# Half passes of three units in one group, and one pool of six banks, in a fused spectral filter and gated MLP kernel

## The chip, the cores and the metric

The kernel runs on one core of one Trainium2 chip. A core has five engines that run side by side and wait for each other by semaphores: TensorE (matrix multiplications), VectorE and ScalarE (elementwise work), GpSimd, and SyncE, which issues the DMA transfers. TensorE writes its results into eight accumulation banks (128 partitions of 512 float32 each, the kernel's PSUM pool); VectorE and ScalarE read them out of there. The metric is the time of one execution in device microseconds.

## The reference

```python
xn = layernorm(x)                                   # x: 2048 x 448, over the last axis
A  = irfft2(rfft2(xn) * (w_r + 1j * w_i))           # 2D FFT filter
gate, up = xn @ W_gate, xn @ W_up                   # 448 -> 1792
B  = ((gate * (gate > 0)) * up) @ W_down            # 1792 -> 448
return x + A + B
```

All in float32. The kernel keeps that accuracy with float16 multiplications by splitting each operand into a high and a low half and adding three products (high by high, high by low, low by high).

## The kernel before

**The MLP.** The 1792 hidden features are 14 blocks f of 128, in three groups (`GROUPS` = 5, 5, 4 blocks). The 2048 rows are four chunks q of 512, worked in the order 0, 2, 1, 3 (`CHUNKS`). A *unit* is one block of one chunk: its gate and its up matrix of 128 x 512 results, each in a bank of its own. With the halves, the 448 contracted features need 10 full passes (128 contracted rows, `gu_full`, L714) and one half pass (64 contracted rows, `gu_half`, L721) for gate, and as many for up. So a unit is 20 full and 2 half passes. The half pass of gate uses the upper 64 rows of the array (`TOP[0]`), that of up the lower 64 (`TOP[1]`), and the two run side by side as a pair.

Half passes are collected: units are taken two at a time. The first of the two, here called the *head*, does its 20 full passes (`gu_unit`), and then `gu_halves` opens the second unit's tile, the *mate*, does the mate's two half passes as its first contributions and the head's two as its last. The mate's 20 full passes follow later and complete it. `tc.high_priority` and a dependency that only fixes an order (`NOSYNC`) keep the four half passes together.

After a unit, ScalarE applies the ReLU to gate (`gu_relu`, L751), VectorE multiplies by up (`gu_times`, L755), ScalarE makes the float16 high part (`gu_hi`, L759), VectorE the low part (`gu_lo`, L763). The unit's banks are free when `gu_relu` and `gu_times` have read them. When all blocks of a group have been done for a chunk, four *down* units follow (`dn_mm`, L782), one for each 128 rows; each adds up 15 or 12 passes in a bank, and VectorE adds the result to `xy` (`dn_post`, L788). The list `units` puts the four down units behind the next pair that ends.

**Banks.** `gu` is a tile of two banks with two buffers, `dn` a tile of one bank with two buffers, and `fx` (for the transforms) another with two: 4 + 2 + 2 = 8.

**Weights.** Each block's weights are loaded, scaled and split by `w_sq`, `w_sum`, `w_scale`, `w_hi` (L664) and `w_lo` (L668), four gate/up units before the block's first unit. A half pass reads the last tile of the low part. The transposed activations `Tq[q]` come by transposing DMAs (`ln_dma`, L332).

**The spectral part** is the *background* work: a list `bg` of some 400 small steps (normalization, DFT matmuls `f_dft` L360, `f_sdft` L392, `i_sdft` L611, `i_ddft` L632, butterflies on VectorE, swap transfers `swap`, L553 reading them). It is spread over the units by a planner: a unit offers VectorE time (`room`) of share x `took` (4.55 us for a gate/up unit, 0.56 us per block for a down unit) less what the unit itself needs (`fixed`, 1.37 or 0.68 us and the weights' work). A bisection finds the share with which the rooms of all units from `RAMP` up to `last_gu` take in the whole list. `run_bg` then issues as many steps behind each unit as its room allows.

**The order of the work.** The first units, up to `hp4` and what stands around it, follow an order written out by hand (`OPENING`). Behind it a list scheduler orders each engine's instructions when the program is built, by priority (order in the program, with `gu_post` and `dn_post` 400 places ahead, `at` steps 200, the half passes behind the first 2000) and by when it expects operands and banks to be there; on the chip every engine then runs its list in order. So a matmul that waits for a bank holds up all matmuls behind it.

Of the kernel before, what the change touches and what calls it, by code (L numbers as in the profile page):

```python
# [21 lines left out]
XW = 4 * GW  # L22
# [119 lines left out]
def tile_gfnet_reglu(ctx: ExitStack, tc: tile.TileContext, x, xr, wgu, wd, wf, wrow, ident, c_fd, c_fm, c_im, c_row, c_id,  # L142
# [9 lines left out]

    def fx():
        return psum.tile([128, 512], F32, name="fx", bufs=2)

# [178 lines left out]
    def ln_tp(n2, tiles):  # L334
        if n2 not in tp:
            tp[n2] = fx().bitcast(F16).rearrange("p (a b) -> p a b", b=128)
        for a in tiles:
            P.transpose(tp[n2][:, a, :], tt[n2][:, a, :], id_t)
# [8 lines left out]


    zps, eo, X, Xh, yps, cur = {}, {}, {}, {}, {}, {}

    def f_dft(n2):
        q, j = n2 % 4, n2 // 4
        js = slice(128 * j, 128 * (j + 1))
        ps = fx()
        T = Tq[q]

        for r in range(4):
            a, b = (r, 4 + r) if r < 3 else (7, 8)
            for i, (t, c) in enumerate(((a, 0), (a, 1), (b, 0))):
                P.matmul(ps[:, r * GW:(r + 1) * GW], T[:, t, js], fd_t[:, r, c], start=(r == 0 and i == 0),  # L360
                         stop=True, skip_group_check=True)
        zps[n2] = ps
# [25 lines left out]
    def f_sdft(n2):  # L388
        y = yps[n2] = fx()[:, 0:XW].rearrange("p (g c k) -> p g c k", g=4, c=2)
# [177 lines left out]
    def row_dft(d):  # L567
        y = state["rowps"] = fx()
# [35 lines left out]
    def i_sdft(n2):  # L604
        ps = fx()
        v, m = vt[n2 % 8][:, n2 // 8], im_t[n2 % 8][:, n2 // 8]
# [19 lines left out]
    def i_ddft(n2):  # L626
        ps = fx()
        h = pgh[n2]
# [79 lines left out]
    def gu_open(f, q):  # L708
        hps[f, q] = psum.tile([128, 2, 512], F32, name="gu", bufs=2)

    def gu_full(f, q, gs, cs, start, stop, seq=SEQ):
        for g in gs:
            for i, (a, b) in enumerate(seq):
                last["P"] = P.matmul(hps[f, q][:, g, cs], wt[f, g][:, a, :], Tq[q][:, b, cs],  # L714
                                     start=(start and i == 0), stop=(stop and i == len(seq) - 1)).ins

    def gu_half(f, q, g, start, prev):


        rows, b = TOP[g]  # L720
        m = P.matmul(hps[f, q][:, g, 0:512], wt[f, g][rows, 7, :], Tq[q][rows, b, :], start=start, stop=not start).ins  # L721
        if "opened" in state:
# [5 lines left out]

    def gu_unit(f, q, mate):

# [5 lines left out]
        gu_full(f, q, gs, cs, True, False)  # L736
        gu_halves(f, q, mate)

    def gu_halves(f, q, mate):
        gu_open(*mate)  # L740
        m = last["P"]
        for i in range(4):
            with tc.high_priority(offset=2000 if i else 0):
                m = gu_half(*((f, q) if i > 1 else mate), 1 - i % 2, i < 2, m)
        opened.add(mate)

    g1s = {}

    def gu_relu(f, q):
        g1s[f, q] = mt([128, 512], F32, "g1", 3)  # L750
        last["A"] = A.activation(g1s[f, q], hps[f, q][:, 0, :], AF.Relu, scale=2.0 ** -22).ins  # L751

    def gu_times(f, q):
        g1 = g1s[f, q]
        last["V"] = V.scalar_tensor_tensor(g1, hps[f, q][:, 1, :], 2.0 ** -22, g1, op0=OP.mult, op1=OP.mult).ins  # L755

# [209 lines left out]
    units += pend  # L966
    mates = {u: v for u, v in zip(gseq[::2], gseq[1::2])}
    first = {}
# [77 lines left out]
    def gu_slab(f, g):  # L1046
        if f % 2 == 0 and g == 0:
            gu_open(f, q)
        gu_full(f, q, (g,), slice(0, 512), f % 2 == 0, f % 2 == 1)

    for f in groups[0]:
# [6 lines left out]
        for tag, fn in (("re", gu_relu), ("tm", gu_times), ("gh", gu_hi), ("gl", gu_lo)):  # L1058
            piece(f"{tag}{f}", fn, f, q)
        if f % 2 == 0:  # L1060
            piece(f"hp{f}", gu_halves, f, q, mates["gu", 0, f, q][2:])
        for g in range(2):
# [11 lines left out]
    with tc.manual_schedule(engines={mybir.EngineType.PE, mybir.EngineType.DVE, mybir.EngineType.Activation,  # L1074
                                     mybir.EngineType.SP, mybir.EngineType.Pool}):
        A.activation(mt([128, 1], F32, "root"), eps, AF.Sqrt)
        G.memset(warm, 0.0)
        wps = psum.tile([128, 512], F32, name="dn", bufs=2)
        gu_open(0, q)
# [17 lines left out]

    last_gu = max(gus) - 6
    lo, hi = 0.3, 1.2
# [13 lines left out]
    for i, u in list(enumerate(units))[len(groups[0]):]:  # L1113
        is_gu = u[0] == "gu"
        if is_gu:
            _, g, f, q = u
            run_bg(until=marks["T", q])
            gu_unit(f, q, (mates.get(u) or (0, 0, None, None))[2:])
        else:
# [70 lines left out]
```

## Time and profile before

| what | value |
|---|---|
| time, median of three runs | 448.41 us (447.95 to 448.84) |
| span of the profiled execution, first to last instruction | 446.9 us |
| TensorE clock granted | 1.000 of full |
| TensorE busy | 437.4 us, 98% |
| VectorE busy | 373.0 us, 83% |
| ScalarE busy | 178.7 us, 40% |

For the profiled execution only its span is given; the 1.5 us between it and the median of the runs lie outside the first and last instruction. In the rows that the prediction shows, a group of instructions is named by its line, engine, operation and tiles (result <- operands), then shapes, the count, the busy time, the mean length of one in ns, and the idle time of the engine just before them with what ended it. In rows of a timeline the first number is the start and the second the length in us from the first start to the last end. Matmuls overlap in their pipeline, so lengths add up to more than the time that passes: the difference of two starts is what a stretch takes.

### The profile page before, as it was taken

The page shows a single profiled execution, that of the slowest core. Times are in us where ns is not written, and L with a number is a line of the kernel's source. Part 1 is how long each engine was busy: PE and PEld are TensorE (multiplying, and loading weights), DVE is VectorE, ACT ScalarE, POOL GpSimd, SP SyncE. Part 2 cuts the span into 40 slices and gives each one's busy share as a digit, 9 for nine tenths or more (in the row PEclk, how much of TensorE's full clock was granted, in tenths as well). Part 3 has the DMA queues.
Part 4 walks back from the last instruction along what each step waited for, and adds up shares of the span by engine and source line. Part 5 has one row for each costly group of instructions (what it writes and reads, how often), then busy time and mean ns, then how long its engine had stood idle before and what let it go on. Part 6 is the DMA issues. An engine that isn't in the chain of part 4 may idle for free.

```text
span 446.9 us, 7057 instructions
## 1 busy us (share of the span) xinstructions
PE 437.4 (98%) x2618; PEld 217.6 (49%) x2618; DVE 373.0 (83%) x801; ACT 178.7 (40%) x365; POOL 35.5 (8%) x100
## 2 busy tenths in 40 slices
PE   7999999999999999999999999999999999999996
PEld 2543545444545444444444444444444456546564
DVE  5988696998859989899999999896997998656474
ACT  5886242451543666043224145434142242233230
POOL 2431031040000150000000010000000000000000
PEclk9999999999999999999999999999999999999999
DMA  7919976041001261431220021000001332121113
GB/s 243 362 38 266 359 243 118 1 94 38 0 14 61 96 219 37 129 103 64 82 77 11 1 83 54 0 13 0 14 0 42 106 96 74 54 76 53 64 43 123
DMA packets 36827, 39.66 MB, mean 89 GB/s; under 512 B 17799, under 2 KB 32185, under 8 KB 36793
## 3 DMA queue, kind: packets, MB, share of 16 engines
q1 hardware_dynamic: 36792, 39.21, 28.1%
q8 instruction: 20, 0.33, 0.3%
q14 instruction: 15, 0.11, 0.1%
HBM read 24.45 MB, written 3.67 MB: 63 GB/s over the span
## 4 chain that ended last, share of the span: by engine, by line
PE 84%; DVE 7%; DMA 4%; ACT 1%; issue 1%; POOL 1%; SPq 1%; DVEq 0%; ACTq 0%
PE gu L714 47%; PE dn L782 27%; PE gu L721 3%; PE fx L360 2%; PE fx L392 2%; DMA sw<-y 2%; PE fx L611 2%; PE fx L632 1%; DMA y<-in_xr 1%; DVE g L755 1%; DMA T<-tt 1%; DVE bst L256 1%; DVE wt L668 1%; DVE xy L788 1%; DVE y L553 1%
## 5 line engine op out<-in xcount | busy, mean ns | idle before, releaser
L714 PE MATMUL gu<-T,wt 128*128 128x512 f16 (+1 forms) x1140 | 256.1, 376 | 0.0
L714 PEld LDWEIGHTS <-wt 128*128 128x128 f16 x1140 | 108.6, 98 | 129.9 <-issue 9.3
L782 PE MATMUL dn<-wdt,h 128*128 128x448 f16 x672 | 136.4, 352 | 0.0
L782 PEld LDWEIGHTS <-h 128*128 128x128 f16 x672 | 64.8, 98 | 60.5
L751 ACT ACTIVATE g<-gu 128x512 f32<-128x512 f32 x56 | 33.2, 594 | 111.0 <-PE gu L721 75.3
L759 ACT ACTIVATE h<-g 128x512 f16<-128x512 f32 x56 | 35.0, 626 | 52.8 <-DVE g L755 52.7
L755 DVE SCALAR_TENSOR_TENSOR g<-gu,g 128x512 f32<-128x512 f32 x56 | 38.3, 684 | 10.3 <-ACT g L751 10.2
L788 DVE SCALAR_TENSOR_TENSOR xy<-dn,dsc,xy 128x448 f32<-128x448 f32 x48 | 32.5, 678 | 15.5 <-PE dn L782 15.3
L763 DVE TENSOR_TENSOR h<-g,h 128x512 f16<-128x512 f32 x56 | 38.2, 684 | 4.9 <-ACT h L759 4.8
L664 ACT ACTIVATE wt<-wst,wsc 128x512 f16<-128x512 f32 x28 | 19.1, 716 | 15.7 <-DVE wsc L204 15.7
L197 POOL PARTITION_ALL_REDUCE wm<-wm x15 | 7.9, 523 | 159.2 <-ACT junk L194 159.2
L668 DVE SCALAR_TENSOR_TENSOR wt<-wst,wsc,wt 128x512 f16<-128x512 f32 x28 | 20.4, 744 | 0.0
L637 DVE SCALAR_TENSOR_TENSOR xy<-fx,fsc,xy 128x448 f32<-128x448 f32 x16 | 10.8, 679 | 10.1 <-PE fx L632 10.1
L721 PE MATMUL gu<-T,wt 64*128 64x512 f16 x112 | 17.0, 381 | 1.7 <-DVE g L755 0.8
L399 DVE TENSOR_TENSOR y<-y 128x456 f32<-128x456 f32 x22 | 13.9, 630 | 4.7 <-DMA row<-y 4.5
L194 ACT ACTIVATE junk<-wst 128x512 bf16<-128x512 f32 x28 | 17.4, 622 | 0.3
L553 DVE TENSOR_TENSOR y<-y,sw 128x456 f32<-128x456 f32 x16 | 10.0, 626 | 8.5 <-DMA sw<-y 8.5
L595 ACT ACTIVATE vt<-y,fsc 128x912 f16<-128x912 f32 x8 | 8.4, 1052 | 20.7 <-PE fx L611 12.3
L618 ACT ACTIVATE wf<-fx 114x512 f16<-114x512 f32 x16 | 9.4, 587 | 17.2 <-PE fx L611 17.0
L398 DVE TENSOR_TENSOR y<-y 128x456 f32<-128x456 f32 x22 | 13.8, 626 | 0.2
L611 PEld LDWEIGHTS <-vt 128*128 128x128 f16 x192 | 12.0, 98 | 3.3
L611 PE MATMUL fx<-wf,vt 128*128 128x128 f16 x192 | 13.2, 219 | 0.0
(115 smaller groups left out, 430.6 us busy)
## 6 DMA issues: line engine op xcount, KB each, us to landing
sw<-y SPq DMA_DIRECT2D x32, 224.4 KB
wst<-in_wgu SPq DMA_DIRECT2D x28, 256.0 KB
wf<-in_wf SPq DMA_DIRECT2D x8, 456.0 KB
y<-in_xr SPq DMA_DIRECT2D x16, 224.0 KB
xy<-in_x SPq DMA_DIRECT2D x16, 224.0 KB
out<-xy SPq DMA_DIRECT2D x16, 224.0 KB
wdst<-in_wd SPq DMA_DIRECT2D x14, 224.0 KB
fm<-in_c_fm SPq DMA_DIRECT2D x8, 128.0 KB
```

The costliest lines, as they stand in the source:

```text
L194: A.activation(o, src, AF.Square, scale=SQ, accum_out=acc)
L611: P.matmul(o, v[:, h, w], m[:, c, :], start=(i == 0), stop=(i == 2), skip_group_check=True)
L664: A.activation(w[:, 0:4, :], wst[f, g], AF.Copy, scale=wsc[f, g])
L668: V.scalar_tensor_tensor(w[:, 4:8, :], st, sc, w[:, 0:4, :], op0=OP.mult, op1=OP.subtract)
L714: last["P"] = P.matmul(hps[f, q][:, g, cs], wt[f, g][:, a, :], Tq[q][:, b, cs], start=(start and i == 0), stop=(stop and i == len(seq) - 1 ...
L721: m = P.matmul(hps[f, q][:, g, 0:512], wt[f, g][rows, 7, :], Tq[q][rows, b, :], start=start, stop=not start).ins
L751: last["A"] = A.activation(g1s[f, q], hps[f, q][:, 0, :], AF.Relu, scale=2.0 ** -22).ins
L755: last["V"] = V.scalar_tensor_tensor(g1, hps[f, q][:, 1, :], 2.0 ** -22, g1, op0=OP.mult, op1=OP.mult).ins
L759: A.activation(ht[f, q][:, 0, :], g1s[f, q], AF.Copy)
L763: V.tensor_tensor(h[:, 1, :], g1s.pop((f, q)), h[:, 0, :], op=OP.subtract)
L782: last["P"] = P.matmul(ps[:, 0:D], ht[f, q][:, a, js], wdt[f][:, b, :], start=(i == 0), stop=(i == n - 1)).ins
L788: last["V"] = V.scalar_tensor_tensor(xy[:, n2, :], dps[n2][:, 0:D], dsc[:, g:g + 1], xy[:, n2, :], op0=OP.mult, op1=OP.add).ins
```

## The change

Units are taken in groups of 2, 2, then sixteen groups of 3, then 2, 2: 20 groups, where there were 28 pairs. A head is followed by one or two mates; after the head's full passes `gu_halves` opens every mate, and four or six half passes stand together, the head's own last. A new order-only dependency puts every later full pass behind the last half pass of the group before. Every unit's gate and up are now two tiles of one bank, and gate, up and down share one pool of six banks; the transforms keep two. The four down units of a finished chunk are put behind the next unit that isn't a head, where they stood behind the next pair's second unit: so at some places they stand between the second and third unit of a group, and at others one unit earlier or later than before. The rooms of the planner end at `max(gus) - 8` where they ended at `max(gus) - 6`. In the opening the same units are heads, and the third group has a second mate.

```diff
-    def fx():
-        return psum.tile([128, 512], F32, name="fx", bufs=2)
+    RINGS = {'gu': ('gu', 6), 'dn': ('gu', 6), 'fx': ('fx', 2)}
+
+    def bank(name="fx"):
+        tag, n = RINGS[name]
+        return psum.tile([128, 512], F32, name=name, tag=tag, bufs=n)
...
     def gu_open(f, q):
-        hps[f, q] = psum.tile([128, 2, 512], F32, name="gu", bufs=2)
+        hps[f, q] = [bank("gu") for g in range(2)]
 
     def gu_full(f, q, gs, cs, start, stop, seq=SEQ):
         for g in gs:
             for i, (a, b) in enumerate(seq):
-                last["P"] = P.matmul(hps[f, q][:, g, cs], wt[f, g][:, a, :], Tq[q][:, b, cs],
+                m = last["P"] = P.matmul(hps[f, q][g][:, cs], wt[f, g][:, a, :], Tq[q][:, b, cs],
                                      start=(start and i == 0), stop=(stop and i == len(seq) - 1)).ins
+                if "opened" in state and "half" in last:
+                    tc.add_manual_dep(m, last["half"].name, NOSYNC, reason="half passes stand together")
...
-    def gu_halves(f, q, mate):
-        gu_open(*mate)
+        gu_halves(f, q, mates)
+
+    def gu_halves(f, q, mates):
         m = last["P"]
-        for i in range(4):
+        vs = [v[2:] for v in mates] + [(f, q)]
+        for i in range(2 * len(vs)):
+            v = vs[i // 2]
+            if i % 2 == 0 and v != (f, q):
+                gu_open(*v)
+                opened.add(v)
             with tc.high_priority(offset=2000 if i else 0):
-                m = gu_half(*((f, q) if i > 1 else mate), 1 - i % 2, i < 2, m)
-        opened.add(mate)
+                m = gu_half(*v, 1 - i % 2, v != (f, q), m)
+        last["half"] = m
...
     def dn_mm(fs, n2):
...
-        ps = psum.tile([128, 512], F32, name="dn", bufs=2)
+        ps = bank("dn")
...
     gseq = [("gu", g, f, q) for g, fs in enumerate(groups) for q in CHUNKS for f in fs]
+    mates, inner, k = {}, set(), 0
+    for n in [2, 2] + [3] * 16 + [2, 2]:
+        mates[gseq[k]] = gseq[k + 1:k + n]
+        inner.update(gseq[k + 1:k + n])
+        k += n
     units, pend = [], []
-    for k, u in enumerate(gseq):
+    for u in gseq:
         units.append(u)
-        if k % 2 and pend:
+        if u in inner and pend:
             units += pend
             pend = []
         if u[2] == groups[u[1]][-1]:
             pend = [("dn", u[1], u[3] + 4 * j, None) for j in range(4)]
     units += pend
-    mates = {u: v for u, v in zip(gseq[::2], gseq[1::2])}
...
-    last_gu = max(gus) - 6
+    last_gu = max(gus) - 8
```

More of the change, by code (lines that the diff above doesn't have):

```diff
@@ L335, in ln_tp @@
         if n2 not in tp:
-            tp[n2] = fx().bitcast(F16).rearrange("p (a b) -> p a b", b=128)
+            tp[n2] = bank().bitcast(F16).rearrange("p (a b) -> p a b", b=128)
         for a in tiles:
@@ L353, in f_dft @@
         js = slice(128 * j, 128 * (j + 1))
-        ps = fx()
+        ps = bank()
         T = Tq[q]
@@ L388, in f_sdft @@
     def f_sdft(n2):
-        y = yps[n2] = fx()[:, 0:XW].rearrange("p (g c k) -> p g c k", g=4, c=2)
+        y = yps[n2] = bank()[:, 0:XW].rearrange("p (g c k) -> p g c k", g=4, c=2)
         m, xh = fm_t[n2 % 8][:, n2 // 8], Xh[n2 % 8][:, n2 // 8]
@@ L567, in row_dft @@
     def row_dft(d):
-        y = state["rowps"] = fx()
+        y = state["rowps"] = bank()
         for d in ((0, 1), (2,))[d]:
@@ L604, in i_sdft @@
     def i_sdft(n2):
-        ps = fx()
+        ps = bank()
         v, m = vt[n2 % 8][:, n2 // 8], im_t[n2 % 8][:, n2 // 8]
@@ L626, in i_ddft @@
     def i_ddft(n2):
-        ps = fx()
+        ps = bank()
         h = pgh[n2]
@@ L713, in gu_full @@
             for i, (a, b) in enumerate(seq):
-                last["P"] = P.matmul(hps[f, q][:, g, cs], wt[f, g][:, a, :], Tq[q][:, b, cs],
+                m = last["P"] = P.matmul(hps[f, q][g][:, cs], wt[f, g][:, a, :], Tq[q][:, b, cs],
                                      start=(start and i == 0), stop=(stop and i == len(seq) - 1)).ins
+                if "opened" in state and "half" in last:
+                    tc.add_manual_dep(m, last["half"].name, NOSYNC, reason="half passes stand together")
     def gu_half(f, q, g, start, prev):
         rows, b = TOP[g]
-        m = P.matmul(hps[f, q][:, g, 0:512], wt[f, g][rows, 7, :], Tq[q][rows, b, :], start=start, stop=not start).ins
+        m = P.matmul(hps[f, q][g], wt[f, g][rows, 7, :], Tq[q][rows, b, :], start=start, stop=not start).ins
         if "opened" in state:
@@ L727, in tile_gfnet_reglu, with gu_unit @@
     opened = set()
-    def gu_unit(f, q, mate):
+    def gu_unit(f, q, mates):
         gs, cs = (0, 1), slice(0, 512)
@@ L750, in gu_relu @@
         g1s[f, q] = mt([128, 512], F32, "g1", 3)
[L751 removed]
+        last["A"] = A.activation(g1s[f, q], hps[f, q][0], AF.Relu, scale=2.0 ** -22).ins
     def gu_times(f, q):
         g1 = g1s[f, q]
[L755 removed]
+        last["V"] = V.scalar_tensor_tensor(g1, hps[f, q][1], 2.0 ** -22, g1, op0=OP.mult, op1=OP.mult).ins
     def gu_hi(f, q):
@@ L1046, in gu_slab @@
     def gu_slab(f, g):
-        if f % 2 == 0 and g == 0:
+        first = ("gu", 0, f, q) in mates
+        if first and g == 0:
             gu_open(f, q)
-        gu_full(f, q, (g,), slice(0, 512), f % 2 == 0, f % 2 == 1)
+        gu_full(f, q, (g,), slice(0, 512), first, not first)
     for f in groups[0]:
@@ L1077, in tile_gfnet_reglu @@
         G.memset(warm, 0.0)
-        wps = psum.tile([128, 512], F32, name="dn", bufs=2)
+        wps = bank("dn")
         gu_open(0, q)
```

7 lines of the change are left out of this document (3 added, 4 removed).

## The prediction

> **What bounds the kernel now.** I read the page's busy shares first, then the chain of work that ended last, then the groups of instructions.
>
> ```profile
> span 446.9 us, 7057 instructions
> PE 437.4 (98%) x2618; PEld 217.6 (49%) x2618; DVE 373.0 (83%) x801; ACT 178.7 (40%) x365; POOL 35.5 (8%) x100
> PEclk9999999999999999999999999999999999999999
> PE 84%; DVE 7%; DMA 4%; ACT 1%; issue 1%; POOL 1%; SPq 1%; DVEq 0%; ACTq 0%
> ```
>
> ```profile
> L714 PE MATMUL gu<-T,wt 128*128 128x512 f16 (+1 forms) x1140 | 256.1, 376 | 0.0
> L782 PE MATMUL dn<-wdt,h 128*128 128x448 f16 x672 | 136.4, 352 | 0.0
> L721 PE MATMUL gu<-T,wt 64*128 64x512 f16 x112 | 17.0, 381 | 1.7 <-DVE g L755 0.8 <-DMA T<-tt 0.8 <-DVE wt L668 0.2
> ```
>
> TensorE is busy from end to end at an undisturbed clock and is 84% of the chain. The full gate and up passes and the down passes have no idle time before them; the half passes have 1.7 us in all, and 1.6 of it is two waits. So this change can gain only by making TensorE's own work shorter or by removing those waits, and can lose by making new ones. 16 groups of three and 4 of two replace 28 groups of two; the numbers of full passes (1140), half passes (112) and down passes (672) stay.
>
> **What a group costs.** Next I read TensorE's timeline: starts, lengths, and the start of whatever follows.
>
> ```profile
> 106.12 2.11 PE L714 MATMUL gu<-T,wt 128*128 128x512 f16 x9
> 108.16 0.61 PE L721 MATMUL gu<-T,wt 64*128 64x512 f16 x4
> 108.70 4.49 PE L714 MATMUL gu<-T,wt 128*128 128x512 f16 x20
> 113.03 1.38 PE L360 MATMUL fx<-fd_t,T 128*128 128x114 f16 x24
> 114.24 4.48 PE L714 MATMUL gu<-T,wt 128*128 128x512 f16 x20
> 118.65 0.61 PE L721 MATMUL gu<-T,wt 64*128 64x512 f16 x4
> 119.19 1.39 PE L360 MATMUL fx<-fd_t,T 128*128 128x114 f16 x24
> 120.42 4.48 PE L714 MATMUL gu<-T,wt 128*128 128x512 f16 x20
> 124.73 0.54 PE L782 MATMUL dn<-wdt,h 128*128 128x448 f16 x2
> ```
>
> A window inside the first of these groups shows its second pair alone:
>
> ```profile
> 108.39 0.38 PE L721 MATMUL gu<-T,wt 64*128 64x512 f16 x2
> ```
>
> Twenty full passes that no half pass follows take 124.73 - 120.42 = 4.31 us, 0.216 each. Twenty that a group follows take 118.65 - 114.24 = 4.41: entering costs 0.10 (nine passes from 106.12 give 2.04 - 1.94 = 0.10 as well). Inside, the second pair starts 108.39 - 108.16 = 0.23 after the first, and the next full pass 108.70 - 108.39 = 0.31 after the second; two half passes of a pair start together, so a pair costs about one full pass, and leaving costs 0.08 more than another pair would. The twenty passes behind a group take 4.33, 0.02 more than undisturbed; I count 0.01.
>
> Edit by edit:
>
> Groups of three. The 56 pairs stay. Eight entries go: 8 x 0.10 = 0.80. Eight exits of 0.31 become steps between pairs of 0.23: 0.64. Eight slowed first passes: 0.08. Together 1.5 us. What the trace doesn't show is the step from a second to a third pair, of which there will be 16. The bounds are a plain pass (0.216, gaining another 0.2) and an exit (0.31, losing 16 x 0.08 = 1.3, so that 0.2 of the gain is left). I take 0.23, since it is the same step between the same instructions. No other engine's time hides this, as TensorE is the chain.
>
> The Trainium skill's "TensorEngine Tiling (Array Packing)", section "Tiling Modes", says that a change of tiling mode drains TensorE, and "TensorE: Matmul & The Clock Gate", section "Step-by-step: what each phase is for", puts the drain at about 128 cycles; two of these a group at 2.4 GHz are an estimate of 0.11 us, and eight groups 0.85 us. The rows give 0.19 a group, nearly twice that, and they decide.
>
> Six banks for gate, up and down. Before, two tiles of two banks served gate and up, and two banks served down. A head's matmuls and a mate's half passes each waited for a whole tile, that is for the multiplication L755 of two units earlier. The one place where it was late:
>
> ```profile
> 397.22 1.46 PE L714 MATMUL gu<-T,wt 128*128 128x512 f16 x6
> 399.49 0.61 PE L721 MATMUL gu<-T,wt 64*128 64x512 f16 x4 [0.81 <-DVE g L755]
> ```
>
> ```profile
> 397.66 0.63 DVE L553 TENSOR_TENSOR y<-y,sw 128x456 f32<-128x456 f32 x1 [4.27 <-DMA sw<-y]
> 398.21 0.63 DVE L554 TENSOR_TENSOR y<-y,sw 128x456 f32<-128x456 f32 x1
> 398.75 0.69 DVE L755 SCALAR_TENSOR_TENSOR g<-gu,g 128x512 f32<-128x512 f32 x1
> ```
>
> VectorE stood 4.27 us for a swap transfer with L755 queued behind it, and TensorE's half passes, with all later gate and up passes behind them, stood 0.81 us. This is the group of blocks 10 and 11 in chunk 3, a pair in both kernels. In the pool of six it needs four banks while the late unit (block 13, chunk 1) holds two, so nothing waits: -0.8. Next to want the late banks is the down work of the finished chunk, a unit later. I take the whole 0.8; its other end is nothing, if the same transfer is late in front of a group of three.
>
> Half passes two units ahead. The third unit's need for its weights' low part moves ahead by one unit; for blocks 5 to 9 the low parts stand in this row, that is the source line's instructions between 130 and 165 us:
>
> ```profile
> L668 DVE SCALAR_TENSOR_TENSOR wt<-wst,wsc,wt x10: 740/742/744, 140.0 to 161.1; 128x512 f16<-128x512 f32 x10
> ```
>
> The first of them to be wanted in the new order, block 6, is wanted when block 4 of chunk 3 ends:
>
> ```profile
> 157.94 4.48 PE L714 MATMUL gu<-T,wt 128*128 128x512 f16 x20
> 162.25 1.11 PE L782 MATMUL dn<-wdt,h 128*128 128x448 f16 x5
> ```
>
> at 162.25, and by 161.9 the last of all ten is done. Chunk 3's transposes are issued by 99.1 and wanted at 113.0, where block 3 of chunk 1 ends in the timeline above:
>
> ```profile
> L332 SPq DMA_TRANSPOSE T<-tt x16: 1162/1317/1383, 20.2 to 99.1; - x16
> ```
>
> So these cost nothing; with the lead gone, a wait for one L668 is 0.74. The wait on chunk 2's transposes (0.8) stays, as the same group opens there: its third unit belongs to the same chunk.
>
> Order and pace. The extra dependency of full passes on the last half pass is an order on one queue: no wait. A gate and up unit's room is share x 4.55 - 1.37, about 3.3 us of VectorE at a share near 1.03; ending two units sooner hands out 6.6 us earlier, 3% of the 213 that the planner's list sums to (255, less its share of 41 of transform matmuls). It adds no instruction. What hides it is VectorE's free time, by stretches:
>
> ```profile
> 160.00:180.00 20.00, 20.00 (x100) 9.16 (x98) 18.51 (x40) 11.83 (x33) 3.97 (x6) 1.00 0.33 115
> 180.00:200.00 20.00, 20.00 (x102) 9.07 (x101) 19.61 (x44) 5.25 (x9) 0.00 (x0) 1.00 0.35 112
> 200.00:220.00 20.00, 20.00 (x102) 9.27 (x101) 19.86 (x39) 5.21 (x11) 0.00 (x0) 1.00 0.16 54
> 220.00:240.00 20.00, 20.00 (x103) 8.80 (x102) 19.62 (x38) 5.92 (x12) 0.00 (x0) 1.00 0.27 85
> 240.00:260.00 20.00, 20.00 (x102) 9.35 (x100) 18.77 (x39) 7.27 (x18) 0.81 (x2) 1.00 0.07 23
> 260.00:280.00 20.00, 20.00 (x99) 9.21 (x98) 18.75 (x38) 8.65 (x21) 1.64 (x2) 1.00 0.19 55
> 400.00:420.00 20.00, 20.00 (x155) 11.71 (x154) 11.74 (x17) 6.49 (x11) 0.00 (x0) 1.00 0.15 54
> ```
>
> (after the length: TensorE, weight loads, VectorE). At the end there is room. From 160 to 280 VectorE is 93 to 99% busy, and TensorE can hardly run faster than its banks are emptied. I take it that the 1.5 us are lost in these 120 of 447 us: 1.5 x 120 / 447 = 0.4. The ends are 0 and the bank waits priced below.
>
> Sum: -1.5 - 0.8 + 0.4 = -1.9 us on the span of 446.9, so 445.0. The runs shown have a median of 448.41, 1.5 above that span, for what lies around it; I carry this over: 446.5.
>
> **Rivals.**
>
> *The banks come free too late (slower).* A group of three wants all six banks when its head ends, so the multiplication of the unit just before must be over in one unit's time, and no down bank may be in use. Lateness of L755 in the saturated stretch:
>
> ```profile
> 187.26 8.81 PE L714 MATMUL gu<-T,wt 128*128 128x512 f16 x40
> 195.91 3.57 PE L782 MATMUL dn<-wdt,h 128*128 128x448 f16 x18
> 199.41 0.61 PE L721 MATMUL gu<-T,wt 64*128 64x512 f16 x4
> ```
>
> ```profile
> 202.76 0.68 DVE L755 SCALAR_TENSOR_TENSOR g<-gu,g 128x512 f32<-128x512 f32 x1
> ```
>
> Block 9 ends at 195.91 and its L755 at 203.44, 7.5 us later. Today 18 down passes stand behind it. In the new order a head (4.4 us) follows at once and then half passes that want these banks: a wait of 7.5 - 4.4 = 3.1 us. One such wait makes 446.5 + 3.1 = 449.6. It decides from 1.9 + 0.9 = 2.8 us of waits. Against it: block 9's group today passes unharmed because VectorE's order was made to suit TensorE's, and the new order will be made so too; and a prompt multiplication ends far sooner:
>
> ```profile
> 242.67 3.38 PE L782 MATMUL dn<-wdt,h 128*128 128x448 f16 x17
> ```
>
> ```profile
> 243.56 0.69 DVE L755 SCALAR_TENSOR_TENSOR g<-gu,g 128x512 f32<-128x512 f32 x1 [0.25 <-ACT g L751]
> ```
>
> 244.25 - 242.67 = 1.6 us. A worse form: banks handed out strictly in turn would give a head the banks of the unit just before it where down work stands ahead of the third unit, at 7 of the 20 groups: 7 x 1.6 = 11, hence 458. Nothing in the trace shows how they are handed out. Chance 0.18, nearly all of it in the mild form. The tiling page of the Trainium skill, sections "PSUM Bottleneck" and "Gotcha 1: PSUM Pressure", speaks for this rival: packing shortens TensorE's work but not the emptying of banks, and row tiles write to different banks, which raises the pressure on them.
>
> *VectorE sets the pace (no change).* The 0.8 us wait turns up elsewhere, since the swap transfers stay as slow, and 1 us of bank waits is added: -1.5 + 0.4 + 1.0 = -0.1, so 448.3. For it speak the 98% stretches; against it, that the whole kernel has 1.7 us of such idle time now. Chance 0.20.
>
> *The group is torn (slower or no change).* If half of the 16 groups of three have a foreign matmul between their pairs, eight exits and entries return: 8 x 0.19 = 1.5, leaving the 0.8 and -1.5 + 1.5 - 0.8 + 0.4 = -0.4: 448.0. All 28 groups of today are whole: 17.0 / 28 = 0.61 us busy each, the single group's length. Chance 0.05.
>
> *More than forecast.* The third pair costs a plain pass (-0.2), no stretch gives back (-0.4): 445.9; if the transposes' 0.8 goes too, 445.1. Chance 0.12.
>
> **How the numbers follow.** The forecast (445.9 to 447.4) has 0.45, more 0.12, no change 0.20, torn 0.05, late banks 0.18. Two runs of this kernel differ by up to 0.2% (0.9 us), so faster means under 447.5: 0.45 + 0.12 and a little of the others, 0.60; within 0.2% 0.21; slower 0.19. The range runs from 445.3 (below it only the case in which every wait goes) to 449.4, which takes in one late bank almost whole.
>
> **What would show it.** Right: the half passes' row has x112 and about 4 x 0.61 + 16 x 0.84 = 15.9 us busy; six of them take 0.77 us to the next full pass; no idle time above 0.3 us stands before the full passes; the wait of 0.81 is gone. Wrong: idle time before gate, up or half passes released by L755, L751 or L788 of more than 2 us in sum, a step to the third pair near 0.31, or groups of fewer than six half passes in the middle of the kernel.

## The result and the profile after

| | before | after |
|---|---|---|
| median of six runs | 448.49 us (447.95 to 448.84) | 453.84 us (452.55 to 457.50) |
| span of the profiled execution | 446.9 us | 450.8 us |

The ratio over all executions is 1.0129, with a 95% interval of 1.0102 to 1.0156 (the two medians alone give 1.012): the change makes the kernel some 1.3% slower. The forecast was 446.5 us, and 453.84 lies outside its range. The medians are 5.4 us apart and the spans 3.9, so three quarters of the loss are in the profiled execution, which was the fastest one (452.55). The others had a granted TensorE clock of 0.992 to 1.000 (the slowest, 457.50, had the 0.992), and what they lost beyond it is not in this trace.

In the kernel after the change the full passes are L716 (L714 before), the half passes L725 (L721), the multiplication L763 (L755), the down passes L790 (L782), the transform matmuls of the inverse part L613 and L634 (L611, L632), the steps that empty their banks L624 and L639 (L622, L637), and the butterfly that reads the swap transfer L555 (L553).

The span and the chain of waits of the page, and the groups of TensorE and of the butterfly, after:

```profile
span 450.8 us, 7086 instructions
PE 61%; DVE 21%; DMA 9%; ACT 3%; issue 3%; SPq 2%; POOL 1%; DVEq 0%; ACTq 0%
...
L725 PE MATMUL gu<-T,wt 64*128 64x512 f16 x112 | 16.1, 380 | 2.2 <-DVE g L763 1.4 <-DMA T<-tt 0.7 <-DVE wt L670 0.2
L613 PE MATMUL fx<-wf,vt 128*128 128x128 f16 x192 | 13.4, 219 | 2.9 <-DVE wf L624 2.9
L634 PE MATMUL fx<-idc_t,wf 114*128 114x112 f16 x192 | 11.9, 213 | 0.2 <-DVE xy L639 0.2
L362 PE MATMUL fx<-fd_t,T 128*128 128x114 f16 x192 | 11.4, 213 | 0.5 <-DVE eo L374 0.5
L555 DVE TENSOR_TENSOR y<-y,sw 128x456 f32<-128x456 f32 x16 | 10.1, 629 | 16.2 <-DMA sw<-y 14.7 <-DMA sw<-row 1.5
```

The same group of the butterfly before, which the prediction did not show:

```profile
L553 DVE TENSOR_TENSOR y<-y,sw 128x456 f32<-128x456 f32 x16 | 10.0, 626 | 8.5 <-DMA sw<-y 8.5
```

TensorE's share of the chain falls from 84 to 61%; VectorE and the DMA transfers have the difference. The wait of 0.8 for the multiplication in block 13 is gone, and five us of new waits have come: 1.4 before half passes, 3.1 before the inverse part's matmuls, 0.5 before the forward ones. VectorE stands 14.7 us for swap transfers where it stood 8.5.

**The groups do what was said.** TensorE's timeline after, a group of six half passes with the matmuls around it; then its second pair onward alone, from a window that cuts the first two off:

```profile
354.68 0.82 PE L725 MATMUL gu<-T,wt 64*128 64x512 f16 x6
355.44 0.84 PE L613 MATMUL fx<-wf,vt 128*128 128x128 f16 x12
...
161.73 0.82 PE L725 MATMUL gu<-T,wt 64*128 64x512 f16 x6
162.48 4.92 PE L716 MATMUL gu<-T,wt 128*128 128x512 f16 x22
```

```profile
354.91 0.59 PE L725 MATMUL gu<-T,wt 64*128 64x512 f16 x4
```

Six half passes take 355.44 - 354.68 = 0.76 us to the next matmul, and 162.48 - 161.73 = 0.75 to the next full pass, where 0.77 was forecast. The second pair starts 0.23 after the first, as before. With the exit of 0.31 that leaves 0.75 - 0.23 - 0.31 = 0.21 for the step to the third pair: the lower of its two bounds, a plain pass, not the 0.23 taken. Before, 28 groups took 28 x 0.54 = 15.1 us; now 4 x 0.54 + 16 x 0.75 = 14.2, and eight entries and slowed passes fewer save 8 x 0.11 = 0.9: 1.8 us in all.

**What a wait costs.** TensorE's timeline after, at the longest one:

```profile
394.61 0.38 PE L716 MATMUL gu<-T,wt 128*128 128x512 f16 x1
396.84 0.84 PE L613 MATMUL fx<-wf,vt 128*128 128x128 f16 x12 [1.85 <-DVE wf L624]
```

From one start to the other are 2.23 us; the pass itself is worth 0.22 (the prediction's plain pass) and the wait 1.85, so 0.16 are lost beyond the wait. With six new waits and one fewer of the old, that is 5 x 0.16 = 0.8.

The sum is -1.8 (groups) - 0.8 (old wait) + 5.0 (new waits) + 0.8 (beyond them) = +3.2 of the span's +3.9. Of the remaining 0.7, 0.2 lie in the opening (the first half pass starts at 19.50 us, before at 19.31); the rest I have not placed.

**Where the long wait is from.** SyncE's queue, then VectorE's timeline, both after the change and around the same time:

```profile
386.25 0.81 SPq L549 DMA_DIRECT2D sw<-y  x1
387.11 0.77 SPq L550 DMA_DIRECT2D sw<-y  x1
```

```profile
386.73 0.68 DVE L624 SCALAR_TENSOR_TENSOR wf<-fx,wf 114x512 f16<-114x512 f32 x1
391.60 0.63 DVE L555 TENSOR_TENSOR y<-y,sw 128x456 f32<-128x456 f32 x1 [4.18 <-DMA sw<-y]
...
392.69 0.68 DVE L763 SCALAR_TENSOR_TENSOR g<-gu,g 128x512 f32<-128x512 f32 x1
...
395.01 1.17 DVE L603 SCALAR_TENSOR_TENSOR vt<-y,fsc,vt 128x912 f16<-128x912 f32 x1 [0.26 <-PE gu L716]
396.10 0.68 DVE L624 SCALAR_TENSOR_TENSOR wf<-fx,wf 114x512 f16<-114x512 f32 x1
```

The swap is issued at 386.25 as two transfers, and its reader L555 can start at 391.60, 5.3 us later. VectorE's list has two steps (1.3 us) between the issue and the reader, so VectorE stands 4.18 us. The multiplication L763 and the next L624 queue behind it, L624 ends at 396.78, and TensorE's L613 starts at 396.84: it writes into one of the two transform banks, and that bank is free only when L624 has read it. On TensorE's list L613 stands ahead of the next gate and up passes, so those stand too. The prediction showed the same stop of 4.27 us before the change; there it cost TensorE 0.81.

### The profile page after: what moved, and what is told of

Its sections match the earlier page's. It is cut to its first block, busy times and chain, and to the rows that moved or that the text cites. A ratio compares the mean times of both kernels' runs of the same rounds, so it can differ in the third digit from the quotient of the medians.

```text
span 450.8 us, 7086 instructions
## 1 busy us (share of the span) xinstructions
PE 437.9 (97%) x2618; PEld 218.9 (49%) x2618; DVE 375.4 (83%) x801; ACT 177.2 (39%) x365; POOL 39.2 (9%) x100
## 4 chain that ended last, share of the span: by engine, by line
PE 61%; DVE 21%; DMA 9%; ACT 3%; issue 3%; SPq 2%; POOL 1%; DVEq 0%; ACTq 0%
PE gu L716 34%; PE dn L790 19%; DMA sw<-y 5%; PE gu L725 2%; DVE g L763 2%; PE fx L394 2%; PE fx L362 2%; PE fx L634 1%; DVE xy L796 1%; PE fx L613 1%; DVE bst L259 1%; DVE vt L603 1%; DMA y<-in_xr 1%; DVE wt L670 1%; DVE y L556 1%
## 5 line engine op out<-in xcount | busy, mean ns | idle before, releaser
L716 PE MATMUL gu<-T,wt 128*128 128x512 f16 (+1 forms) x1140 | 252.9, 376 | 0.0
L716 PEld LDWEIGHTS <-wt 128*128 128x128 f16 x1140 | 108.9, 98 | 128.8 <-issue 6.8
L790 PE MATMUL dn<-wdt,h 128*128 128x448 f16 x672 | 132.3, 353 | 0.0
L790 PEld LDWEIGHTS <-h 128*128 128x128 f16 x672 | 65.0, 98 | 59.4
L763 DVE SCALAR_TENSOR_TENSOR g<-gu,g 128x512 f32<-128x512 f32 x56 | 38.3, 684 | 10.6 <-ACT g L759 6.6
L555 DVE TENSOR_TENSOR y<-y,sw 128x456 f32<-128x456 f32 x16 | 10.1, 629 | 16.2 <-DMA sw<-y 14.7
L200 POOL PARTITION_ALL_REDUCE wm<-wm x15 | 6.9, 461 | 153.9 <-ACT junk L197 153.9
L725 PE MATMUL gu<-T,wt 64*128 64x512 f16 x112 | 16.1, 380 | 2.2 <-DVE g L763 1.4
L639 DVE SCALAR_TENSOR_TENSOR xy<-fx,fsc,xy 128x448 f32<-128x448 f32 x16 | 10.8, 680 | 7.4 <-PE fx L634 7.3
L385 ACT ACTIVATE Xh<-X 128x912 f16<-128x912 f32 x8 | 7.7, 961 | 21.7 <-DVE X L383 21.7
L613 PE MATMUL fx<-wf,vt 128*128 128x128 f16 x192 | 13.4, 219 | 2.9 <-DVE wf L624 2.9
## 6 DMA issues: line engine op xcount, KB each, us to landing
wf<-in_wf SPq DMA_DIRECT2D x8, 456.0 KB
```

What stands on the lines that cost most here:

```text
L613: P.matmul(o, v[:, h, w], m[:, c, :], start=(i == 0), stop=(i == 2), skip_group_check=True)
L716: m = last["P"] = P.matmul(hps[f, q][g][:, cs], wt[f, g][:, a, :], Tq[q][:, b, cs], start=(start and i == 0), stop=(stop and i == len(seq) ...
L725: m = P.matmul(hps[f, q][g], wt[f, g][rows, 7, :], Tq[q][rows, b, :], start=start, stop=not start).ins
L763: last["V"] = V.scalar_tensor_tensor(g1, hps[f, q][1], 2.0 ** -22, g1, op0=OP.mult, op1=OP.mult).ins
L790: last["P"] = P.matmul(ps[:, 0:D], ht[f, q][:, a, js], wdt[f][:, b, :], start=(i == 0), stop=(i == n - 1)).ins
```

## Experiments: the change in parts

Three short edits make nearly all of them: the pace (`last_gu = max(gus) - N`, 6 before, 8 after), the sizes of the groups, and the banks (`RINGS`). Two theories run through the expectations: that one part of the change brings the waits (the pool, the groups, or the rooms that end earlier), and that any edit makes the list scheduler write other orders for the engines, of which the kernel before has an unusually good one. The expectations call them B (the pool), G (the groups), P (the pace, that is the rooms) and, from the second set on, O (the order).

**e1_pace_undone**, the kernel after with the old pace:

```diff
-    last_gu = max(gus) - 8
+    last_gu = max(gus) - 6
```

> The changed kernel with the rooms of the background work ending at max(gus) - 6 again; groups of three and the pool of six stay. Theory P (the pace: background work comes two units sooner, its transform matmuls stand in TensorE's queue ahead of gate and up passes and wait for VectorE, which waits for swap transfers): most of the 3.6 us of such waits go, time 448 to 450.5. Theory G (a group of three needs all six banks at once): nothing changes, 452.5 to 454.5. Theory B (the shared pool itself, without down banks of its own): nothing changes, 452.5 to 454.5.

459.68 us, ratio 1.0232 (1.0206 to 1.0257). None of the three theories had this. The pace alone isn't what makes the change slow: with the old pace it loses 11 us, not 5. Some 4.8 of them went, in the profiled execution, with a TensorE clock that was halved for a while after its waits, as the section on the hardware shows.

**e2_pace_alone**, the kernel before with the new pace:

```diff
-    last_gu = max(gus) - 6
+    last_gu = max(gus) - 8
```

> The kernel before with the rooms ending at max(gus) - 8, nothing else. Theory P: slower, 450.5 to 452.5, with waits of transform matmuls (L611, L632) for VectorE of 2 to 4 us after 350 us. Theories G and B: as before, 448 to 449.

451.16 us, ratio 1.0056 (1.0036 to 1.0076). Theory P expected this (450.5 to 452.5), but was wrong about e1: the pace that helps the kernel after costs the kernel before 2.4 us. The parts do not add up.

**e3_banks_alone**, the kernel after with pairs and the old pace, and **e4_banks_pace**, the same with the new pace. Both keep two other things of the change, the tiles of one bank and the new order-only dependency, so they are not the pool alone. The edit that they share:

```diff
-    for n in [2, 2] + [3] * 16 + [2, 2]:
+    for n in [2] * 28:
```

> Groups of two as before and the pace of before, but gate, up and down in one pool of six single banks. Theories P and G: 447.5 to 448.7 (the wait of 0.81 for L755 may go). Theory B: slower already, 450 to 453.

> The changed kernel with groups of two: pool of six and the new pace. Theory P: slower, 450.5 to 453. Theory G: not slower, 447.5 to 448.7. Theory B: slower, 450 to 453, the same as with the pool alone.

453.83 us, 1.0109 (1.0091 to 1.0126), and 455.06 us, 1.0142 (1.0127 to 1.0157). The pool of six with pairs, which gains nothing from longer groups, loses as much as the whole change, and groups of three can't be the cause there. e3's groups, after the opening:

```profile
L725 PE MATMUL gu<-T,wt 64*128 64x512 f16 x112 | 17.0, 381 | 0.9 <-DMA T<-tt 0.7 <-DVE wt L670 0.2
...
L634 PE MATMUL fx<-idc_t,wf 114*128 114x112 f16 x192 | 11.9, 212 | 2.6 <-DVE wf L624 1.9 <-DVE xy L639 0.8
```

No half pass waits for a bank here; the inverse part's matmuls wait, as in the kernel after.

## Experiments: is it the banks, or the written order?

If sharing the banks were the cause, pairs that keep the old four, two and two banks in single tiles would be as fast as before; if any edit costs, a change of the pace by one unit would cost too.

**n1_pace7** and **n2_pace5**, the kernel before with one number changed:

```diff
-    last_gu = max(gus) - 6
+    last_gu = max(gus) - 7      # n2_pace5: - 5
```

> The kernel before with the rooms of the background ending one unit sooner (max(gus) - 7), nothing else. Theory O (order: any change of the program lets the scheduler write other lists, and each list but a selected one has 2 to 10 us of waits on the chip, because swap transfers take longer than the lists allow for): 450 to 455 although the edit is next to nothing. Theory P (pace costs in proportion): about halfway to the 451.2 of two units, 449.5 to 450.2. Theory B (the shared pool is the cause): 448.3 to 449.2.

> The kernel before with the rooms ending one unit later (max(gus) - 5). Theory O: 450 to 455. Theory P: a little faster, 447 to 448.5. Theory B: 448.3 to 449.2.

451.92 us, 1.0074 (1.0057 to 1.0091), and 456.01 us, 1.0170 (1.0147 to 1.0194). A step of one unit either way, with not one operation more or fewer, costs 3.2 and 7.3 us (theory O had 450 to 455, and n2 lies above it). The traces show the other orders: of TensorE's 2618 instructions 2121 stand in n1 in the same sequence as before, and of VectorE's 801 only 601. The groups and then the two timelines of n2:

```profile
L714 PE MATMUL gu<-T,wt 128*128 128x512 f16 (+1 forms) x1140 | 255.6, 375 | 2.0 <-DVE g L755 2.0
L632 PE MATMUL fx<-idc_t,wf 114*128 114x112 f16 x192 | 11.9, 212 | 2.4 <-DVE wf L622 1.8 <-DVE xy L637 0.6
L553 DVE TENSOR_TENSOR y<-y,sw 128x456 f32<-128x456 f32 x16 | 10.1, 628 | 16.1 <-DMA sw<-y 15.2 <-DMA sw<-row 0.9
```

```profile
394.08 0.63 DVE L553 TENSOR_TENSOR y<-y,sw 128x456 f32<-128x456 f32 x1 [4.04 <-DMA sw<-y]
...
395.18 0.68 DVE L755 SCALAR_TENSOR_TENSOR g<-gu,g 128x512 f32<-128x512 f32 x1
```

```profile
395.92 1.46 PE L714 MATMUL gu<-T,wt 128*128 128x512 f16 x6 [2.02 <-DVE g L755]
```

The same picture as after the change, in a kernel with the old banks and pairs: VectorE stands 4.04 us for a swap, the multiplication queues behind it, TensorE stands 2.02 us. Its stops for swaps are 15.2 us in sum.

**n3_split_own**, pairs, old pace, tiles of one bank but nothing shared, and **n4_five_three**, pairs, old pace, five banks for gate, up and down and three for the transforms:

```diff
-    RINGS = {'gu': ('gu', 6), 'dn': ('gu', 6), 'fx': ('fx', 2)}
+    RINGS = {'gu': ('gu', 4), 'dn': ('dn', 2), 'fx': ('fx', 2)}      # n3_split_own
+    RINGS = {'gu': ('gu', 5), 'dn': ('gu', 5), 'fx': ('fx', 3)}      # n4_five_three
```

> Groups of two and the pace of before; gate and up are two tiles of one bank in a pool of four, and down keeps two banks of its own, so nothing is shared. Theory B (down work and units compete for one pool): as before, 448 to 449. Theory O: 450 to 455, like the shared pool's 453.8, since this edit too makes the scheduler write other lists.

> Groups of two and the pace of before; gate, up and down share five banks, the transforms have three. If the two transform banks bound the inverse part (one step from i_sdft to i_acc every 6.1 us after 375 us), the steps come at 4 to 5 us and the waits of transform matmuls for L624 go: 446 to 449. If it is bound by the swap transfers and VectorE's order (theory O): steps stay near 6 us, 450 to 455.

n3 took 454.94 us, 1.0133 (1.0115 to 1.0152). Without any sharing it is 6.2 us slower, so sharing isn't needed for the loss. It is not a clean case: seven of its groups are torn, and it too has the tiles of one bank and the new dependency. n4 took 451.61 us, 1.0061 (1.0046 to 1.0076), 2.2 less than e3 with one bank fewer for gate, up and down. Where the emptying of the inverse part's banks starts and ends, in n4 and before (the source line's instructions: durations in ns, first and last start):

```profile
L639 DVE SCALAR_TENSOR_TENSOR xy<-fx,fsc,xy x16: 673/676/685, 370.6 to 425.0; 128x448 f32<-128x448 f32 x16
```

```profile
L637 DVE SCALAR_TENSOR_TENSOR xy<-fx,fsc,xy x16: 673/679/685, 366.6 to 441.0; 128x448 f32<-128x448 f32 x16
```

With a third bank the last one starts 16 us earlier, although the first starts 4 us later; in e3, which differs from n4 in the banks alone, they run from 369.9 to 447.2. So in the orders of e3 and of the kernel before, the two banks draw the inverse part out to the kernel's end. A third loosens it, but n4 still has waits (1.4 at L613, 1.0 before down passes) and does not beat the kernel before.

## Experiments: without the inverse part, without its swaps

**i1_noinv_two** and **i2_noinv_three** leave out the inverse transforms of the filter (A is not added) in the kernel before and after:

```diff
-        for t in range(16 + 6 + len(il)):
+        for t in range(0):
...
+    stored = set(range(16))
```

> The kernel before without the inverse transforms: the last loop of the background list (the last butterflies U, swap, pair, i_sdft to i_acc) is left out, and the down work alone is added to x, so the output lacks the inverse filter. TensorE loses 384 passes (about 20 us). Both theories: about 426 to 430, as the reference for the next run.

> The changed kernel with the same part left out. Theory O (the loss sits in the inverse part's waits and in the lists around it; the groups themselves save their 1.7 us): 1 to 2.5 us faster than the run of two units with the same part left out. Theory G or B (groups of three or the pool cost waits in the gate and up stage): equal or slower than it by up to 5 us.

428.57 us, 0.9555 (0.9541 to 0.9569), and 429.15 us, 0.9569 (0.9554 to 0.9583). Of the 5.4 us that the change costs, 0.6 is left. That speaks for the inverse part as the place of most of the loss, though both kernels got new orders with this edit. The gain of the groups, which theory O expected to show through here, is missing too. i2's groups:

```profile
L716 PE MATMUL gu<-T,wt 128*128 128x512 f16 (+1 forms) x1140 | 250.1, 375 | 1.2 <-ACT zc L369 1.2
...
L725 PE MATMUL gu<-T,wt 64*128 64x512 f16 x112 | 16.3, 380 | 1.4 <-DMA T<-tt 0.7 <-DVE g L763 0.5 <-DVE wt L670 0.2
```

A wait of 1.2 in the forward part and one of 0.5 for a bank eat most of it. With i1's own wait of 0.6 before down passes (L782), about 0.9 us of the difference between the two is not placed.

**i3_noswap_two** and **i4_noswap_three** keep every step but leave out the large swap transfers of the inverse part (its butterflies read what stands in the tile from before), in the kernel before and after:

```diff
     def swap(...):
+        if key == "U":
+            return
```

> The kernel before without the big swap transfers of the inverse part (the exchange of mirrored rows is left out there, so the filter's result is wrong; all other work stands). Theory O with late swaps as its cause: no wait of VectorE for them, 446 to 448.5. If lists err for other reasons too: 448.5 to 453.

> The changed kernel with the same swap transfers left out. Theory O with late swaps as its cause: the waits of 3.6 us after 350 us go, 446 to 449, at or below the kernel of two units without them. If the lists err for other reasons (VectorE's and ScalarE's own lengths): 450 to 455 as the changed kernel.

448.15 us, 0.9989 (0.9979 to 0.9999; a tenth execution took 463.55 us and is not counted), and 450.25 us, 1.0033 (1.0015 to 1.0050). i4's groups:

```profile
L727 PE MATMUL gu<-T,wt 64*128 64x512 f16 x112 | 16.1, 380 | 1.9 <-DVE g L765 1.1 <-DMA T<-tt 0.7 <-DVE wt L672 0.2
L615 PE MATMUL fx<-wf,vt 128*128 128x128 f16 x192 | 13.2, 219 | 0.0
L636 PE MATMUL fx<-idc_t,wf 114*128 114x112 f16 x192 | 11.9, 212 | 0.0
L362 PE MATMUL fx<-fd_t,T 128*128 128x114 f16 x192 | 11.4, 213 | 1.7 <-DVE eo L374 1.7
```

This is the clearest pair, because the orders hardly change: TensorE's 2618 instructions stand in i4 exactly as in the kernel after, and 797 of VectorE's 801 do; in i3 it is 2613 and 799, against the kernel before. So here the swap transfers alone are taken away. They cost the kernel before about 0.5 us and the kernel after about 3.6: with them gone, no inverse matmul waits. Of the 5.4 us lost, 2.1 stay (450.25 - 448.15), so i4 misses the 446 to 449 expected with late swaps as the whole cause. A bank wait of 1.1 and 1.7 in the forward part, with what is lost beyond them, less the 1.8 that the groups save, make 1.5 of it.

## Experiments: other draws of the three-unit kernel

**j1_three_p7** and **j2_three_p10** are the kernel after at paces 7 and 10; **j3_five_three_p4** and **j4_five_three_p2** are n4 at paces 4 and 2 (only `last_gu` differs).

> The changed kernel with the rooms ending at max(gus) - 7, one unit later; nothing else. Theory O (each edit draws new lists, and the change's loss is one such draw): anything from 450 to 460, not between its neighbours 453.8 (at - 8) and 459.7 (at - 6), and the waits stand at other places but for the bank wait near 190 us. If the pace itself sets the loss: 456 to 457.5.

> The changed kernel with the rooms ending at max(gus) - 10, two units sooner. Theory O: 449 to 460, unordered. If the pace itself sets the loss (459.7, 453.8 at - 6 and - 8): 447 to 449.

> Groups of two, five banks for gate, up and down, three for the transforms, the rooms ending at max(gus) - 4. With a third bank the inverse part ended 16 us before the kernel's end, so a slower pace is to be had: fewer VectorE steps per unit ahead of L755. If the lists' luck decides: 449 to 455; if the slack covers the swap transfers: 446.5 to 449.

> The same with the rooms ending at max(gus) - 2. If the lists' luck decides: 449 to 455; if the slack covers the swap transfers: 446.5 to 449.

450.69 us, 1.0057 (1.0038 to 1.0077); 464.51 us, 1.0354 (1.0329 to 1.0378); 450.67 us, 1.0049 (1.0031 to 1.0068); 449.86 us, 1.0030 (1.0017 to 1.0042). j1's half passes, and j2's inverse matmuls:

```profile
L725 PE MATMUL gu<-T,wt 64*128 64x512 f16 x112 | 16.9, 380 | 2.5 <-DVE g L763 1.6 <-DMA T<-tt 0.7 <-DVE wt L670 0.2
```

```profile
L613 PE MATMUL fx<-wf,vt 128*128 128x128 f16 x192 | 13.8, 225 | 5.2 <-DVE xy L639 4.6 <-DVE wf L624 0.6
L634 PE MATMUL fx<-idc_t,wf 114*128 114x112 f16 x192 | 12.9, 222 | 4.1 <-DVE wf L624 3.2 <-DVE xy L639 0.8
```

j1 is the best three-unit kernel with the sizes of the change: its inverse part runs without a wait, and the new wait that is left is for a bank (1.6). j2, outside theory O's 449 to 460, crowds the inverse part: the emptying L639 runs from 358.6 to 414.4 there (366.0 to 443.8 after the change), TensorE waits 9.3 us in sum at L613 and L634 for L624 and L639, which empty the two transform banks, and one group is torn. j3 and j4 have the third bank and a slower pace, and lie in the range given for the lists' luck, not in the one for slack that covers the swaps.

**k1_mixed_p8** and **k2_mixed_p7** put pairs where j1 and the kernel after wait for the bank, at paces 8 and 7:

```diff
-    for n in [2, 2] + [3] * 16 + [2, 2]:
+    for n in [2, 2] + [3] * 5 + [2, 2, 2] + [3] * 9 + [2, 2]:
```

> The changed kernel with the two groups of three at blocks 4 (chunk 3) to 9 (chunk 0) taken as three groups of two, 21 groups in all; pace as changed (- 8). If a group of three is what makes the wait for L763 near 188 us (all six banks wanted at once): that wait is gone. For the rest theory O: 449 to 460, since the lists are new again.

> The same at the pace - 7, where the groups of three had the wait near 189 us (1.59) as their only one after the opening, at 450.7. If the wait goes and the lists stay as good: 448 to 449. Theory O: 449 to 460.

k1 took 451.87 to 456.68 us in three executions, 1.0128 (1.0078 to 1.0178); the fourth, which was the one profiled, took 930.7 us, so no trace of k1 is read. k2 took 451.46 us, 1.0051 (1.0031 to 1.0071). k2's timeline at the next group of three:

```profile
201.97 0.60 PE L725 MATMUL gu<-T,wt 64*128 64x512 f16 x3
204.23 0.59 PE L725 MATMUL gu<-T,wt 64*128 64x512 f16 x3 [1.66 <-DVE g L763]
```

The wait near 188 is gone, 1.66 us stand at 204 in its place, and another 1.05 at 114.6, where j1 has none. Pairs at one spot only move it.

The draws by pace and form, median us (the kernel before lies at 448.5 to 448.8 in each comparison; n3 and the mixed k1 and k2 have forms of their own):

| pace | pairs, own banks | groups of three, pool of six | pairs, pool of six | pairs, five and three banks |
|---|---|---|---|---|
| 2 | | | | 449.9 |
| 4 | | | | 450.7 |
| 5 | 456.0 | | | |
| 6 | 448.5 (before) | 459.7 | 453.8 | 451.6 |
| 7 | 451.9 | 450.7 | | |
| 8 | 451.2 | 453.8 (after) | 455.1 | |
| 10 | | 464.5 | | |

At equal pace, groups of three stand 11.2 us above pairs with their own banks (6, where a halved clock has part of it), 1.2 below (7) and 2.7 above (8). The sign of the comparison depends on the pace, that is on which order the scheduler happens to write. No draw beats the kernel before.

## Why the prediction was wrong

**Groups: right.** -1.5 was forecast, -1.8 measured; the third pair costs the lower bound. The busy time of the half passes is 16.1 us, forecast 15.9, and the group was not torn.

**Six banks: the wait went, the gain didn't stay.** No gate, up or half pass waits any more at the place of the 0.81. That the late multiplication was only one thing in a queue behind a swap was in the quoted rows; the swap stayed, and what queued behind it next was L624. I gave this to the rival in which the wait turns up elsewhere, with the right mechanism, at a price of 1.0 us and a chance of 0.20. It measured 3.6 (3.1 at the inverse matmuls, 0.5 at the forward ones; the 0.5 doesn't hang on the inverse part's swaps, since i4 has 1.7 there without them). Which edit of the change made the swaps more costly the runs don't tell: e3, n2 and e1 all have it, with different edits.

**Weights, transposes: right.** The waits before half passes for them are 0.7 and 0.2, as before.

**Late banks: the rival was right in kind, and too dear.** It priced one wait of 7.5 - 4.4 = 3.1 us. After the change, VectorE's and TensorE's timelines have it one group earlier than the example:

```profile
178.96 0.63 DVE L555 TENSOR_TENSOR y<-y,sw 128x456 f32<-128x456 f32 x1 [2.98 <-DMA sw<-y]
...
188.15 0.68 DVE L763 SCALAR_TENSOR_TENSOR g<-gu,g 128x512 f32<-128x512 f32 x1
```

```profile
186.89 0.60 PE L725 MATMUL gu<-T,wt 64*128 64x512 f16 x3
188.88 0.59 PE L725 MATMUL gu<-T,wt 64*128 64x512 f16 x3 [1.39 <-DVE g L763]
```

VectorE stood 2.98 us for a swap and then had a full list until the multiplication. The unit before the head ended about 186.89 - 4.41 = 182.5, its multiplication at 188.83, 6.3 us later; less the head's 4.4 and the 0.5 for the three half passes that had their banks, 1.4 remain. I argued against it that the new order would be made to suit TensorE, as the old one was. The scheduler did not place the multiplication in time. The worse form of the rival, banks that make heads wait at seven places, did not come: the full passes wait nowhere. Such a wait, of 0.5 to 2.6 us between 185 and 205 us, stands in each of the seven three-unit profiles read (after, e1, i2, i4, j1, j2, k2) and in none of the five of pairs that share banks (e3, e4, n4, j3, j4). n3, pairs that share nothing, has two there (0.84 before full passes, 0.58 before half passes). So this is the one cost that goes with groups of three in these runs, though pairs can have it too. The tiling page of the Trainium skill, "TensorEngine Tiling (Array Packing)", section "Gotcha 1: PSUM Pressure", says that row tiles write to different banks and so raise the pressure on them; this row agrees.

**The step that failed is "Order and pace".** It said that the edit adds no instruction, that VectorE's free time hides it, and from 11.74 busy of 20 us between 400 and 420 that "at the end there is room". The 0.4 us that it charged went to the stretch from 160 to 280. But that row lies behind the last swap: the last butterfly before the change starts at 398.21, and VectorE's idle time from 400 to 420 was ended by TensorE and ScalarE alone. The stretch ahead of it, before the change, looks as roomy by its busy time (after the length: TensorE, weight loads, VectorE, ScalarE):

```profile
380.00:400.00 20.00, 19.19 (x149) 10.47 (x146) 11.49 (x20) 4.38 (x7) 0.00 (x0) 1.00 0.22 72
```

Here 7.3 of VectorE's 8.5 idle us are two stops for swap transfers, of 2.99 and 4.27. While it stands so, in its written order, it has no room for anything that is listed behind. From 340 us on these stops came to 7.3 us before the change and 11.5 after. The stretch that I called saturated gave one wait of 1.4 us; the inverse part's stretch, which I took for roomy, gave 3.1 of the 5.0, at starts from 357 to 397 us. So a term of 0.4 us stood where new waits of 5.0, with 0.8 lost beyond them, were measured. My signs of being wrong did not cover them either: they named waits before gate, up and half passes, which came to 1.4 us. That the pace edit alone could cost anything was priced from 0 to the bank waits of the first rival; e2, n1 and n2 measured 2.4, 3.2 and 7.3 us, with stops of VectorE ahead of the longest waits, and the step had no term for an order written anew.

**What stays open.** i3 and i4 show, at almost unchanged orders, that 3.3 of the 5.4 us hang on the swaps. They don't show that the new form must meet them worse: j1 is the same form without a wait in the inverse part, and n2 the old form with waits in it. How much of the change's loss is the form and how much the order that this build drew can't be separated with these runs; the bank wait alone stands in every three-unit draw that was read, and in j1, where it is the only new wait and two groups are torn, the kernel is still 2.0 us slower than before; 1.0 of that lies behind the last matmul, whose start is 5.0 us ahead of the span's end there and 4.0 before. No run has the old groups and banks with the new dependency alone.

## What to carry to other kernels

Before a low busy share is counted as room, read what ended that engine's idle time: an engine that stands in a fixed order for a transfer delays everything listed behind it. Where orders are written when the kernel is built, measure first how far neutral edits move the time (here 2 to 7 us for one to two units of pace), since a gain of 2 us worked out from instructions is smaller than that spread, and a well-drawn order can be lost with any edit. A removed wait should be followed to its cause: if the late thing stays late, ask what is next in its queue.

## What the runs showed of the hardware

A wait can cost more than its length. e1's timeline at its bank wait, and then TensorE, weight loads, VectorE, ScalarE and GpSimd busy, the granted clock and the DMA share by stretches of it:

```profile
186.91 0.60 PE L725 MATMUL gu<-T,wt 64*128 64x512 f16 x3
190.09 1.01 PE L725 MATMUL gu<-T,wt 64*128 64x512 f16 x3 [2.58 <-DVE g L763]
```

```profile
185.00:190.00 5.00, 2.51 (x13) 0.80 (x11) 4.17 (x8) 0.00 (x0) 0.00 (x0) 0.95 0.37 121
190.00:195.00 5.00, 4.91 (x13) 1.56 (x13) 5.00 (x17) 1.23 (x2) 0.00 (x0) 0.50 0.35 112
195.00:200.00 5.00, 5.00 (x22) 2.10 (x20) 5.00 (x15) 3.50 (x6) 0.00 (x0) 0.87 0.01 3
200.00:205.00 5.00, 5.00 (x25) 2.24 (x24) 5.00 (x10) 2.30 (x4) 0.00 (x0) 1.00 0.65 184
```

With 0.50 throughout the second stretch, the 0.95 of the first is half a microsecond at half clock and the 0.87 of the third 1.3: half clock for 0.5 + 5.0 + 1.3 = 6.8 us, during and after the wait. In the 5 us of the second stretch TensorE did 13 matmuls, in the fourth 25. The first 0.6 us of the 6.8 lie in the wait itself; half of the other 6.2 is 3.1 us lost on top of the 2.58. "TensorE: Matmul & The Clock Gate" in the Trainium skill, section "What's actually happening", has the half rate follow an idle window of about 3.4 us; the half rate agrees, but here 2.58 us of waiting were enough.

The length of one wait does not decide it alone. The wait of 1.39 us at the same place after the change left the clock at 1.00 in its profile, and so did those of 1.85 us after the change and of 2.02 in n2. But in e1 the clock is halved once more, from about 411.4 to 414.8 us, after waits of 1.32 and 0.85 that left TensorE idle for 2.17 of 3.0 us; there 1.7 us are lost, 4.8 in all. That the same happens in those executions of the changed kernel whose clock was below 1.000 is likely, but no trace shows it.
